# Linear attention, then SwiGLU: batch 0's values by plain loads with casts on chip, smaller first weight slices, and four tiny early reads

## The chip, the cores and the metric

The kernel runs on one core of a Trainium2 chip. Times are device microseconds of one execution of the whole program. A core has five engines with a queue of instructions each: TensorE (PE, with its weight loads shown apart as PEld), VectorE (DVE), ScalarE (ACT), GpSimd (POOL) and SyncE (SP). They run side by side and wait for one another by semaphores. Transfers are issued from the queues of SP, ACT and GpSimd and carried out by 16 DMA engines.

## What is computed

```python
# q, k, v: [8 batches, 8 heads, 576 tokens, 64], float32
q_s = softmax over the 64 of each row of q
k_s = softmax over the 576 tokens of k
kv = einsum('bhsd,bhse->bhde', k_s, v)
attn = einsum('bhsd,bhde->bhse', q_s, kv)
x = attn.transpose(0, 2, 1, 3).reshape(4608, 512)
g = x @ w_gate            # [512, 1536]
out = (g * sigmoid(g) * (x @ w_val)) @ w_out      # [1536, 512]
```

Only the exponentials are taken, without the maximum; the division by the row sum of q is done on q, the one by the column sum of k on the rows of kv.

## The kernel before

**Attention.** A batch is worked in two groups G of four heads. A tile of q, k or v of a group has 128 partitions: partition halves g = 0 and 1 hold head pairs, nine tokens of each head lie in one partition, and the two heads of a pair stand side by side, so a raw tile is 128 x 2 x 576. `load` (L72) brings one in as float32 on the SP queue. `exp_of` takes exponentials on ScalarE into bf16 (`eq`, `ek`); `norm_sum` and `norm_mul` make the normalised q (`qs`) on VectorE; `turn_pe` transposes `qs` on PE into PSUM (`tp`) and `turn_out` copies it out (`qt`). The nine token steps are cut in two pieces, `BANKS = ((0, 5), (5, 9))`, of 640 and 512 columns. `kv` is the sum over the nine steps of `ek` transposed times v; it is scaled into `kn`, and `x_mm` multiplies `kn` with `qt` into `xp`, which `x_out` copies into `xt`, the bf16 input of the feed-forward part, [128, 4, 4608].

**Feed-forward.** `m_unit` (L286) makes 128 of the 1536 hidden columns for one batch of tokens: matmuls of `wg` and of `wv` with `xt`, over four slices kk of the model dimension, then Silu on ScalarE (`sg`) and the product on VectorE (`hr`). For batch 0 the 576 tokens stand in two parts of 320 and 256. Slices kk = 0 and 1 of `xt` come from group 0, kk = 2 and 3 from group 1. `o_mm` multiplies `hr` with `wo` for 128 tokens, and the result is copied and stored.

**Order.** Inside `tc.manual_schedule()` (L353) the order of the code is the order of each engine's queue. The opening is written out by hand for batch 0 (L354 to L452):

- SP issues q and k of group 0, then q and k of group 1.
- GpSimd waits until k of group 0 has landed (the manual dependency of L359), then issues the loads of v, which cast float32 to bf16 on the way (`v16`; group 1 in two pieces of tokens). On the same queue follow the weight slices, casting too: columns 0 to 256, 256 to 640, 640 to 1024 and 1024 to 1536 of `wg` and `wv` in turn (L380), then four slices of `wo`.
- ScalarE takes the exponentials; VectorE the sums and the normalised q of group 0, then of group 1.
- PE first does matmuls on zeros (`spin`), which keep it busy, the sums of k over tokens (`key_sum`, whose reciprocal `kvr` VectorE takes), the transposes, `kv_first` (kv of batch 0, from `v16`), `x_mm`, and then the twelve `m_unit`s of batch 0 with PE work alone between them. In the first of these (`by_part`) all matmuls of the first 320 tokens stand ahead of those of the other 256.
- Batch 1's loads are released when the second slice of `wo` has landed (`w_dma[-3]`, L454), batch 2's as buffers come free.

After that the work goes in chunks of about 512 tokens, with the attention of a later batch placed between the `m_unit`s of an earlier one; there v is loaded as float32 on SP and cast on GpSimd (`cast_v`, L127). That part is the same in both kernels.

Of the kernel before, what the change touches and what calls it, by code (L numbers as in the profile page):

```python
# [15 lines left out]
def kernel(  # L16
# [10 lines left out]
    nc = tc.nc  # L27
# [26 lines left out]
    hr = const.tile([128, MT, RING], BF16, name="hr", tag="hr")  # L54
    ident = const.tile([128, 128], BF16, name="ident", tag="ident")
    sel = const.tile([128, 2], BF16, name="sel", tag="sel")
    zero = const.tile([128, 512], BF16, name="zero", tag="zero")
    vbs = [const.tile([128, T, 130], BF16, name=f"vb{i}", tag=f"vb{i}") for i in range(2)]
    v16 = [const.tile([128, 2, T * 64], BF16, name=f"v16_{i}", tag=f"v16_{i}") for i in range(2)]
# [2 lines left out]

    raw = {}

    def head_ap(src, b, G, t0=0, t1=T):
        return bass.AP(
            tensor=src.tensor,
            offset=src[b, 4 * G].offset + 64 * t0,
            ap=[[T * 64, 128], [2 * HSTR, 2], [1, (t1 - t0) * 64]],
        )  # L70

    def load(what, src, b, G, pieces=((0, T),), after=None):  # L72
        t_ = ld.tile([128, 2, T * 64], FP32, tag=what, name=what)
        raw[what, b, G] = t_
        last = None
        for t0, t1 in pieces:
            last = nc.sync.dma_start(out=t_[:, :, 64 * t0:64 * t1], in_=head_ap(src, b, G, t0, t1))
            if after is not None:
                tc.add_manual_dep(last.ins, after.ins.name, SYNC, reason="order of loads")
                after = None  # L80
        return last
# [61 lines left out]
        nc.vector.reciprocal(out=rr, in_=rs)  # L143
        return first

    def norm_mul(b, G, pieces=((0, T),), engs=None):
# [3 lines left out]
        for (t0, t1), eng in zip(pieces, engs or (nc.vector, nc.vector)):  # L150
            n = 2 * (t1 - t0)
            eng.tensor_mul(  # L152
                qs[:, t0:t1, :].rearrange("p t (h d) -> p (t h) d", d=64),
                eq2[:, 2 * t0:2 * t1, :],
                s["rr"][:, 2 * t0:2 * t1].to_broadcast([128, n, 64]),
            )
# [27 lines left out]
    def ek_of(b, G, g, t):  # L184
        return st[b, G]["ek"][64 * g:64 * g + 64, t, :, :].rearrange("p h d -> p (h d)")
# [49 lines left out]
    def x_one(b, G):  # L235
        for i in range(2):
            x_out(b, G, i, x_mm(b, G, i))
# [45 lines left out]

    def m_unit(c0, n, m, by_part=False):  # L286
        ms = slice(m * 128, (m + 1) * 128)
        parts = [(c0, n)] if n <= 512 else [(c0, 320), (c0 + 320, n - 320)]
        gu = []
        for nm in ("g_ps", "u_ps"):  # L290
            ps = [bank(nm) for _ in parts]
            gu.append(ps)
        steps = [(a, kk, i) for a in range(2) for kk in range(KT) for i in range(len(parts))]
        if by_part:
            steps.sort(key=lambda a: (a[2], a[0], a[1]))
        for a, kk, i in steps:
            c, w_ = parts[i]
            nc.tensor.matmul(  # L298
                out=gu[a][i][:, 0:w_], lhsT=(wg, wv)[a][:, kk, ms], rhs=xt[:, kk, c:c + w_],
                start=(kk == 0), stop=(kk == KT - 1),  # L300
            )
# [49 lines left out]

    make_identity(nc, ident)
    with tc.manual_schedule():  # L353
        kd = []  # L354
        for G in range(NG):
            load("q", q, 0, G)
            kd.append(load("k", k, 0, G))
        d = nc.gpsimd.dma_start(out=v16[0], in_=head_ap(v, 0, 0))  # L358
        tc.add_manual_dep(d.ins, kd[0].ins.name, SYNC, reason="order of loads")  # L359
        for t0, t1 in BANKS:  # L360
            nc.gpsimd.dma_start(out=v16[1][:, :, 64 * t0:64 * t1], in_=head_ap(v, 0, 1, t0, t1))  # L361

        warm = const.tile([128, 1], FP32, name="warm", tag="warm")
        nc.vector.memset(warm, 0.0)
# [11 lines left out]
        first = norm_sum(0, 0, BANKS)  # L376
        norm_mul(0, 0, BANKS)
        norm_sum(0, 1, BANKS)

        for c0, n in ((0, 256), (256, 384), (640, 384), (1024, 512)):  # L380
            w_slice(wg, moe_w_gate, c0, n)
            w_slice(wv, moe_w_val, c0, n)
        w_dma = [wo_slice(m0, 3) for m0 in (0, 3, 6, 9)]
# [17 lines left out]
            s["kvr"] = at.tile([128, 2], FP32, tag="kvr", name="kvr")  # L401
            nc.vector.reciprocal(out=s["kvr"], in_=ks[:, 0:2])

        def kv_first(G, t0=0, t1=T):
            s = st[0, G]
            if t0 == 0:
                s["kv"] = [bank("kv") for _ in range(2)]
            for t in range(t0, t1):
                for g in range(2):
                    r = slice(64 * g, 64 * g + 64)  # L410
                    nc.tensor.matmul(
                        out=s["kv"][g][:, 0:128].rearrange("p (h d) -> p h d", d=64),
                        lhsT=ek_of(0, G, g, t), rhs=v16[G][r, :, 64 * t:64 * t + 64],
                        start=(t == 0), stop=(t == T - 1),
                    )

        def scale_first(G, eng1):
            s = st[0, G]
            kn = s["kn"] = at.tile([128, 2, 128], BF16, tag="kn1", name="kn1")
            nc.scalar.mul(kn[:, 0, :], s["kv"][0][:, 0:128], s["kvr"][:, 0:1])  # L420
            if eng1 is nc.scalar:
                nc.scalar.mul(kn[:, 1, :], s["kv"][1][:, 0:128], s["kvr"][:, 1:2])
            else:
                nc.vector.tensor_scalar_mul(kn[:, 1, :], s["kv"][1][:, 0:128], s["kvr"][:, 1:2])

        spin(8)
        spin(6, first)
        key_sum(0)
        turn_pe(0, 0, 0)
        turn_pe(0, 0, 1)  # L430
        turn_out(0, 0, 0, nc.scalar)
        exp_of("k", 0, 1)
        turn_out(0, 0, 1, nc.scalar)
        norm_mul(0, 1, BANKS)
        spin(6)
        key_sum(1)
        kv_first(0)
        scale_first(0, nc.scalar)
        turn_pe(0, 1, 0)
        turn_pe(0, 1, 1)  # L440
        turn_out(0, 1, 0, nc.vector)
        turn_out(0, 1, 1, nc.vector)
        xp0 = x_mm(0, 0, 0), x_mm(0, 0, 1)
        kv_first(1, *BANKS[0])
        kv_first(1, *BANKS[1])
        x_out(0, 0, 0, xp0[0], (nc.scalar, nc.scalar))
        x_out(0, 0, 1, xp0[1], (nc.vector, None))
        scale_first(1, nc.vector)
        xp1 = x_mm(0, 1, 0), x_mm(0, 1, 1)
        x_out(0, 1, 0, xp1[0], (nc.scalar, nc.vector))  # L450
        x_out(0, 0, 1, xp0[1], (None, nc.vector))
        x_out(0, 1, 1, xp1[1], (nc.scalar, nc.vector))  # L452

        load_batch(1, w_dma[-3], by_group=True)  # L454
        load_batch(2)

        for m in range(MT):
            m_unit(0, S, m, by_part=(m == 0))

        exp_of("q", 1, 0)  # L460
        exp_of("k", 1, 0)
# [121 lines left out]
```

## Time and profile before

| | |
|---|---|
| time, median of 3 runs | 317.82 us (317.57 to 317.85) |
| the profiled execution | 317.75 us, span 316.0 us |
| PE busy | 304.7 us, 96% of the span |
| DVE, ACT, POOL busy | 52%, 47%, 9% |
| DMA moved | 45.75 MB, 145 GB/s on average |
| granted TensorE clock | 0.998 |

The span is the time from the first to the last instruction on the core, and somewhat shorter than the timed run. PE is busy in 96% of it, but matmuls are pipelined and their ends are modelled, so that "busy" is not "at its peak". In the page's 40 slices of 7.9 us PE is at 90% or more from the third slice to the last but one; the first two have 60 and 70%. What lies ahead of the third slice, the first 16 us, is the opening for batch 0 described above. DMA is busy at 70 to 90% of its share in the first seven slices, and clearly less later.

### The profile page before, as it was taken

Reading aid. Unit: us, or ns where it says so; the run is one execution under the profiler, and the core shown is the slowest. Engines: PE = TensorE matmul, PEld = TensorE weight load, DVE = VectorE, ACT = ScalarE, POOL = GpSimd, SP = SyncE. Lnnn points to the kernel's source line nnn. Section 1 sums busy time; section 2 is a strip of 40 time slices with the busy share of each in tenths; the row PEclk is TensorE's granted clock in tenths of the full one; section 3 lists DMA queues with packets and bytes.
Section 4 is the critical chain, followed back from the end, with each engine's and each line's share of the span. In section 5 each row is a group of like instructions: output and inputs, shape, how many; then the busy total and the mean of one; then the engine's idle time right before and its main releaser. Section 6 shows DMA issues by size and latency. Waiting matters only on the chain.

```text
span 316.0 us, 4856 instructions
## 1 busy us (share of the span) xinstructions
PE 304.7 (96%) x1865; PEld 152.0 (48%) x1894; DVE 163.2 (52%) x277; ACT 147.6 (47%) x218; POOL 28.0 (9%) x35
## 2 busy tenths in 40 slices
PE   6799999999999999999999999999999999999994
PEld 2477744554444444544454444544454444444443
DVE  3834476685754566455835492639354333423421
ACT  4743488634663465447354637355743113312300
POOL 2930021100200020002000200020000000000000
PEclk9999999999999999999999999999999999999999
DMA  7999999269246806490629253944310202020124
GB/s 269 183 204 207 296 393 391 68 160 364 50 91 179 338 17 128 112 394 11 141 68 352 97 110 66 322 162 103 66 41 0 65 3 66 0 68 3 31 68 102
DMA packets 39304, 45.75 MB, mean 145 GB/s; under 512 B 16368, under 2 KB 23024, under 8 KB 39280
## 3 DMA queue, kind: packets, MB, share of 16 engines
q1 hardware_dynamic: 32480, 39.99, 42.0%
q0 software_dynamic: 6640, 5.31, 10.9%
q8 instruction: 15, 0.25, 0.3%
q10 hardware_dynamic: 160, 0.13, 0.2%
q14 instruction: 9, 0.07, 0.1%
HBM read 37.75 MB, written 9.44 MB: 149 GB/s over the span
## 4 chain that ended last, share of the span: by engine, by line
PE 88%; DMA 4%; DVE 3%; ACT 2%; issue 1%; POOL 1%; SPq 0%; DVEq 0%
PE g_ps L298 29%; PE u_ps L298 29%; PE o_ps L322 25%; PE kv L191 3%; DMA wv<-in_moe_w_val_dram 2%; DMA k<-in_k_dram 2%; DVE rs L138 1%; PE xp L267 1%; DVE qs L152 1%; PE o_ps L342 1%; ACT L124 1%; ACT eq L124 1%; POOL v L361 0%; PE tp L166 0%; POOL v L358 0%
## 5 line engine op out<-in xcount | busy, mean ns | idle before, releaser
L305 ACT ACTIVATE sg<-g_ps 128x512 bf16<-128x512 f32 (+2 forms) x120 | 65.1, 554 | 139.1 <-PE g_ps L298 120.7
L306 DVE TENSOR_TENSOR hr<-sg,u_ps 128x512 bf16<-128x512 bf16 (+2 forms) x120 | 74.5, 630 | 87.8 <-PE u_ps L298 80.4
L298 PE MATMUL g_ps<-xt,wg 128*128 128x512 bf16 (+2 forms) x469 | 110.0, 358 | 1.0 <-ACT xt L111 0.2
L298 PE MATMUL u_ps<-xt,wv 128*128 128x512 bf16 (+2 forms) x468 | 109.8, 357 | 1.2 <-DMA wv<-in_moe_w_val_dram 0.5
L322 PE MATMUL o_ps<-wo,hr 128*128 128x512 bf16 x414 | 93.0, 379 | 0.4 <-issue 0.2
L298 PEld LDWEIGHTS <-wv 128*128 128x128 bf16 x480 | 46.9, 98 | 47.2 <-DMA wv<-in_moe_w_val_dram 0.9
L298 PEld LDWEIGHTS <-wg 128*128 128x128 bf16 x480 | 45.8, 98 | 45.3 <-issue 0.7
L322 PEld LDWEIGHTS <-hr 128*128 128x128 bf16 x420 | 40.9, 98 | 49.1
L113 DVE COPY o_sb<-o_ps 128x512 f32<-128x512 f32 x33 | 22.4, 680 | 39.2 <-PE o_ps L322 37.3
L127 POOL CAST vb<-v 128x1152 bf16<-128x1152 f32 x14 | 16.0, 1146 | 174.3 <-DMA v<-in_v_dram 111.8
L138 DVE TENSOR_REDUCE rs<-eq 128x18 f32<-128x1152 bf16 (+2 forms) x18 | 21.7, 1214 | 13.2 <-ACT eq L124 13.2
L152 DVE TENSOR_TENSOR qs<-eq,rr 128x1152 bf16<-128x1152 bf16 (+2 forms) x18 | 22.1, 1237 | 0.1
L124 ACT ACTIVATE eq<-q 128x1152 bf16<-128x1152 f32 (+2 forms) x18 | 18.1, 1050 | 4.5 <-DMA q<-in_q_dram 4.4
L124 ACT ACTIVATE ek<-k 128x1152 bf16<-128x1152 f32 x16 | 18.0, 1158 | 0.3 <-DMA k<-in_k_dram 0.2
L305 ACT ACT_TABLE_LOAD x12 | 15.4, 1283 | 0.2
L124 ACT ACT_TABLE_LOAD x11 | 14.1, 1283 | 0.2
L388 PE MATMUL idle<-zero 128*128 128x512 bf16 x20 | 6.1, 459 | 3.0 <-DVE rs L138 1.8
L191 PE MATMUL kv<-vb,ek 64*128 64x129 bf16 x252 | 8.7, 217 | 0.0
L191 PEld LDWEIGHTS <-ek 64*128 64x128 bf16 x252 | 7.3, 94 | 2.7 <-ACT sg L305 2.1
L275 ACT CAST xt<-xp 128x512 bf16<-128x512 f32 x12 | 6.4, 588 | 3.6 <-PE xp L267 3.6
L276 DVE CAST xt<-xp 128x512 bf16<-128x512 f32 x12 | 7.7, 683 | 0.0
L347 ACT COPY o_sb<-o_ps 128x128 f32<-128x128 f32 x2 | 0.5, 265 | 13.3 <-DVE o_sb L346 13.3
(46 smaller groups left out, 70.2 us busy)
## 6 DMA issues: line engine op xcount, KB each, us to landing
q<-in_q_dram SPq DMA_DIRECT2D x16, 576.0 KB, 5.6
k<-in_k_dram SPq DMA_DIRECT2D x16, 576.0 KB, 7.3
out_dram<-o_sb SPq DMA_DIRECT2D x70, 128.0 KB, 2.3
v<-in_v_dram SPq DMA_DIRECT2D x14, 576.0 KB, 9.0
wo<-in_moe_w_out_dram POOLq DMA_DIRECT2D x4, 384.0 KB, 16.3
wg<-in_moe_w_gate_dram POOLq DMA_DIRECT2D x2, 384.0 KB, 9.7
wv<-in_moe_w_val_dram POOLq DMA_DIRECT2D x2, 384.0 KB, 10.7
wg<-in_moe_w_gate_dram POOLq DMA_DIRECT2D x1, 512.0 KB, 13.7
```

The lines of the kernel that those rows point to most:

```text
L113: eng.tensor_copy(out=out, in_=in_)
L124: nc.scalar.activation(out=e[:, t0:t1], in_=src[:, t0:t1], func=AF.Exp)
L127: nc.gpsimd.tensor_copy(out=vbs[G][:, :, 0:128].rearrange("p t (h d) -> p t h d", d=64), in_=raw["v", b, G].rearrange("p h (t d) -> p t h ...
L138: i = nc.vector.reduce_sum(out=rs[:, 2 * t0:2 * t1], in_=eq2[:, 2 * t0:2 * t1, :], axis=mybir.AxisListType.X)
L152: eng.tensor_mul(qs[:, t0:t1, :].rearrange("p t (h d) -> p (t h) d", d=64), eq2[:, 2 * t0:2 * t1, :], s["rr"][:, 2 * t0:2 * t1].to_broadca ...
L191: nc.tensor.matmul(out=kv[g][:, c:c + 129], lhsT=ek_of(b, G, g, t), rhs=vbs[G][r, t, 0:129], start=(t == 0), stop=(t == T - 1),)
L275: nc.scalar.copy(out=xt[:, 2 * G, c0:c0 + 512], in_=main[G][0])
L276: nc.vector.tensor_copy(out=xt[:, 2 * G + 1, c0:c0 + 512], in_=main[G][1])
L298: nc.tensor.matmul(out=gu[a][i][:, 0:w_], lhsT=(wg, wv)[a][:, kk, ms], rhs=xt[:, kk, c:c + w_], start=(kk == 0), stop=(kk == KT - 1),)
L305: nc.scalar.activation(out=sg[:, 0:w_], in_=g_ps[:, 0:w_], func=AF.Silu)
L306: nc.vector.tensor_mul(hr[:, m, r:r + w_], sg[:, 0:w_], u_ps[:, 0:w_])
L322: nc.tensor.matmul(out=o_ps, lhsT=hr[:, m, r0:r0 + 128], rhs=wo[:, m, :], start=(m == 0), stop=(m == MT - 1),)
```

## The change

- **v of batch 0** is no longer cast by its DMA. Both groups come in as float32 on the SP queue, like q and k, in the order q0, k0, q1, v0, k1, v1; v1 comes head by head (`by_head`), in two transfers. Group 0 is cast by one copy on GpSimd, which stands ahead of the weight slices on that queue. Group 1 is cast by `cast_half`, one head at a time: 384 columns on VectorE and 192 on ScalarE.
- **Weight slices** of `wg` and `wv` are now columns 0 to 128, 128 to 256, 256 to 512, 512 to 1024 and 1024 to 1536: ten issues instead of eight.
- **Four tiny reads**, 16 rows of 16 numbers each of k, v, `w_gate` and `w_val`, are issued on the ScalarE queue ahead of everything else there. Their destination `touch` is read by nothing.
- **Order on the engines**: `key_sum` moves behind the first transposes (group 0) and behind those of group 1 (group 1); kv of group 1 is made head by head (`kv_first(1, 0, 1)` and `kv_first(1, 1, 2)`), each behind the cast of its half; `kn` of group 0 is scaled by ScalarE and VectorE, one half each, instead of by ScalarE alone; the copies of `xp` and `qt` stand in another order.
- **First `m_unit`**: the sort takes kk = 0 and 1 (both parts, `wg` and `wv`) ahead of kk = 2 and 3.

An argument of `norm_mul` that no call uses goes as well; that hunk is left out.

```diff
--- before
+++ after
@@ -54,6 +54,7 @@
     hr = const.tile([128, MT, RING], BF16, name="hr", tag="hr")
     ident = const.tile([128, 128], BF16, name="ident", tag="ident")
     sel = const.tile([128, 2], BF16, name="sel", tag="sel")
+    touch = const.tile([16, 4, 16], FP32, name="touch", tag="touch")
     zero = const.tile([128, 512], BF16, name="zero", tag="zero")
     vbs = [const.tile([128, T, 130], BF16, name=f"vb{i}", tag=f"vb{i}") for i in range(2)]
     v16 = [const.tile([128, 2, T * 64], BF16, name=f"v16_{i}", tag=f"v16_{i}") for i in range(2)]
@@ -62,19 +63,19 @@
 
     raw = {}
 
-    def head_ap(src, b, G, t0=0, t1=T):
+    def head_ap(src, b, G, h=(0, 2)):
         return bass.AP(
             tensor=src.tensor,
-            offset=src[b, 4 * G].offset + 64 * t0,
-            ap=[[T * 64, 128], [2 * HSTR, 2], [1, (t1 - t0) * 64]],
+            offset=src[b, 4 * G + 2 * h[0]].offset,
+            ap=[[T * 64, 128], [2 * HSTR, h[1] - h[0]], [1, T * 64]],
         )
 
-    def load(what, src, b, G, pieces=((0, T),), after=None):
+    def load(what, src, b, G, after=None, by_head=False):
         t_ = ld.tile([128, 2, T * 64], FP32, tag=what, name=what)
         raw[what, b, G] = t_
         last = None
-        for t0, t1 in pieces:
-            last = nc.sync.dma_start(out=t_[:, :, 64 * t0:64 * t1], in_=head_ap(src, b, G, t0, t1))
+        for h in ((0, 1), (1, 2)) if by_head else ((0, 2),):
+            last = nc.sync.dma_start(out=t_[:, h[0]:h[1], :], in_=head_ap(src, b, G, h))
             if after is not None:
                 tc.add_manual_dep(last.ins, after.ins.name, SYNC, reason="order of loads")
                 after = None
@@ -283,7 +284,7 @@
 
 
 
-    def m_unit(c0, n, m, by_part=False):
+    def m_unit(c0, n, m, first=False):
         ms = slice(m * 128, (m + 1) * 128)
         parts = [(c0, n)] if n <= 512 else [(c0, 320), (c0 + 320, n - 320)]
         gu = []
@@ -291,8 +292,8 @@
             ps = [bank(nm) for _ in parts]
             gu.append(ps)
         steps = [(a, kk, i) for a in range(2) for kk in range(KT) for i in range(len(parts))]
-        if by_part:
-            steps.sort(key=lambda a: (a[2], a[0], a[1]))
+        if first:
+            steps.sort(key=lambda a: (a[1] // 2, a[2], a[0], a[1]))
         for a, kk, i in steps:
             c, w_ = parts[i]
             nc.tensor.matmul(
@@ -351,14 +352,18 @@
 
     make_identity(nc, ident)
     with tc.manual_schedule():
-        kd = []
-        for G in range(NG):
-            load("q", q, 0, G)
-            kd.append(load("k", k, 0, G))
-        d = nc.gpsimd.dma_start(out=v16[0], in_=head_ap(v, 0, 0))
-        tc.add_manual_dep(d.ins, kd[0].ins.name, SYNC, reason="order of loads")
-        for t0, t1 in BANKS:
-            nc.gpsimd.dma_start(out=v16[1][:, :, 64 * t0:64 * t1], in_=head_ap(v, 0, 1, t0, t1))
+        load("q", q, 0, 0)
+        load("k", k, 0, 0)
+        load("q", q, 0, 1)
+        load("v", v, 0, 0)
+        load("k", k, 0, 1)
+        load("v", v, 0, 1, by_head=True)
+        for i, src in enumerate((k, v, moe_w_gate, moe_w_val)):
+            row = src.shape[-1] if len(src.shape) == 2 else 8 * T * 64
+            nc.scalar.dma_start(
+                out=touch[:, i, :],
+                in_=bass.AP(tensor=src.tensor, offset=src[(0,) * len(src.shape)].offset, ap=[[row, 16], [1, 16]]),
+            )
 
         warm = const.tile([128, 1], FP32, name="warm", tag="warm")
         nc.vector.memset(warm, 0.0)
@@ -376,8 +381,9 @@
         first = norm_sum(0, 0, BANKS)
         norm_mul(0, 0, BANKS)
         norm_sum(0, 1, BANKS)
-
-        for c0, n in ((0, 256), (256, 384), (640, 384), (1024, 512)):
+        nc.gpsimd.tensor_copy(out=v16[0], in_=raw["v", 0, 0])
+
+        for c0, n in ((0, 128), (128, 128), (256, 256), (512, 512), (1024, 512)):
             w_slice(wg, moe_w_gate, c0, n)
             w_slice(wv, moe_w_val, c0, n)
         w_dma = [wo_slice(m0, 3) for m0 in (0, 3, 6, 9)]
@@ -401,61 +407,62 @@
             s["kvr"] = at.tile([128, 2], FP32, tag="kvr", name="kvr")
             nc.vector.reciprocal(out=s["kvr"], in_=ks[:, 0:2])
 
-        def kv_first(G, t0=0, t1=T):
+        def kv_first(G, h0=0, h1=2):
             s = st[0, G]
-            if t0 == 0:
+            if h0 == 0:
                 s["kv"] = [bank("kv") for _ in range(2)]
-            for t in range(t0, t1):
+            for t in range(T):
                 for g in range(2):
                     r = slice(64 * g, 64 * g + 64)
                     nc.tensor.matmul(
-                        out=s["kv"][g][:, 0:128].rearrange("p (h d) -> p h d", d=64),
-                        lhsT=ek_of(0, G, g, t), rhs=v16[G][r, :, 64 * t:64 * t + 64],
+                        out=s["kv"][g][:, 64 * h0:64 * h1].rearrange("p (h d) -> p h d", d=64),
+                        lhsT=ek_of(0, G, g, t), rhs=v16[G][r, h0:h1, 64 * t:64 * t + 64],
                         start=(t == 0), stop=(t == T - 1),
                     )
 
-        def scale_first(G, eng1):
+        def cast_half(h):
+            n = 64 * 6
+            nc.vector.tensor_copy(out=v16[1][:, h, 0:n], in_=raw["v", 0, 1][:, h, 0:n])
+            nc.scalar.copy(out=v16[1][:, h, n:], in_=raw["v", 0, 1][:, h, n:])
+
+        def scale_first(G):
             s = st[0, G]
             kn = s["kn"] = at.tile([128, 2, 128], BF16, tag="kn1", name="kn1")
             nc.scalar.mul(kn[:, 0, :], s["kv"][0][:, 0:128], s["kvr"][:, 0:1])
-            if eng1 is nc.scalar:
-                nc.scalar.mul(kn[:, 1, :], s["kv"][1][:, 0:128], s["kvr"][:, 1:2])
-            else:
-                nc.vector.tensor_scalar_mul(kn[:, 1, :], s["kv"][1][:, 0:128], s["kvr"][:, 1:2])
+            nc.vector.tensor_scalar_mul(kn[:, 1, :], s["kv"][1][:, 0:128], s["kvr"][:, 1:2])
 
         spin(8)
         spin(6, first)
+        turn_pe(0, 0, 0)
         key_sum(0)
-        turn_pe(0, 0, 0)
         turn_pe(0, 0, 1)
         turn_out(0, 0, 0, nc.scalar)
+        turn_out(0, 0, 1, nc.scalar)
         exp_of("k", 0, 1)
-        turn_out(0, 0, 1, nc.scalar)
         norm_mul(0, 1, BANKS)
         spin(6)
-        key_sum(1)
         kv_first(0)
-        scale_first(0, nc.scalar)
         turn_pe(0, 1, 0)
+        scale_first(0)
         turn_pe(0, 1, 1)
         turn_out(0, 1, 0, nc.vector)
+        key_sum(1)
+        cast_half(0)
+        xp0 = x_mm(0, 0, 0), x_mm(0, 0, 1)
         turn_out(0, 1, 1, nc.vector)
-        xp0 = x_mm(0, 0, 0), x_mm(0, 0, 1)
-        kv_first(1, *BANKS[0])
-        kv_first(1, *BANKS[1])
-        x_out(0, 0, 0, xp0[0], (nc.scalar, nc.scalar))
-        x_out(0, 0, 1, xp0[1], (nc.vector, None))
-        scale_first(1, nc.vector)
-        xp1 = x_mm(0, 1, 0), x_mm(0, 1, 1)
-        x_out(0, 1, 0, xp1[0], (nc.scalar, nc.vector))
-        x_out(0, 0, 1, xp0[1], (None, nc.vector))
-        x_out(0, 1, 1, xp1[1], (nc.scalar, nc.vector))
+        kv_first(1, 0, 1)
+        x_out(0, 0, 0, xp0[0])
+        cast_half(1)
+        kv_first(1, 1, 2)
+        scale_first(1)
+        x_out(0, 0, 1, xp0[1])
+        x_one(0, 1)
 
         load_batch(1, w_dma[-3], by_group=True)
         load_batch(2)
 
         for m in range(MT):
-            m_unit(0, S, m, by_part=(m == 0))
+            m_unit(0, S, m, first=(m == 0))
 
         exp_of("q", 1, 0)
         exp_of("k", 1, 0)
```

More of the change, by code (lines that the diff above doesn't have):

```diff
@@ L144, in norm_sum, with norm_mul @@
         return first
-    def norm_mul(b, G, pieces=((0, T),), engs=None):
+    def norm_mul(b, G, pieces=((0, T),)):
         s = st[b, G]
@@ L149, in norm_mul @@
         qs = s["qs"] = at.tile([128, T, 128], BF16, tag="qs", name="qs")
-        for (t0, t1), eng in zip(pieces, engs or (nc.vector, nc.vector)):
+        for t0, t1 in pieces:
             n = 2 * (t1 - t0)
-            eng.tensor_mul(
+            nc.vector.tensor_mul(
                 qs[:, t0:t1, :].rearrange("p t (h d) -> p (t h) d", d=64),
```

## Prediction

> **What bounds the kernel now.** I read the chain of work that ended last first. On the page PE has 88% of it and DMA 4%: nearly the whole span is matmul after matmul, and an edit of the opening can only shift the moment from which that stream runs without gaps. So I asked for the same chain in order of time (start, us, what), over the first 20 us:
>
> ```profile
> 1.27 4.79 DMA k<-in_k_dram
> 6.05 0.30 issue
> 6.36 0.86 POOL v L358
> 7.21 1.43 POOL v L361 x2
> 8.64 0.74 POOL wg L99
> 9.38 6.77 DMA wv<-in_moe_w_val_dram
> 16.15 0.05 issue
> 16.20 0.72 PE u_ps L298 x4
> ```
>
> The first matmuls with wv wait for their weights. GpSimd holds its queue until k of group 0 has landed (6.06), issues three loads of v and then wg and wv, and wv lands at 16.15. After that PE is never idle: the timeline puts the first matmul of unit m=1 at 17.63, and from there each m takes 2 x 0.98 us. **17.63 is the number to compare with.**
>
> Second, the timelines by engine, to see how far behind that DMA the attention of batch 0 is (start, us, engine, line, op, tile, shapes, count, idle before):
>
> ```profile
> 8.94 1.41 DVE L138 TENSOR_REDUCE rs<-eq 128x10 f32<-128x640 bf16 x2 [0.38 <-ACT eq L124]
> 10.38 0.27 DVE L143 RECIPROCAL rr<-rs 128x18 f32<-128x18 f32 x1
> 10.57 0.11 DVE L402 RECIPROCAL kvr<-ks 128x2 f32<-128x2 f32 x1
> 10.69 1.43 DVE L152 TENSOR_TENSOR qs<-eq,rr 128x640 bf16<-128x640 bf16 x2
> 12.03 0.16 DVE L402 RECIPROCAL kvr<-ks 128x2 f32<-128x2 f32 x1
> ...
> 14.38 0.45 PE L220 MATMUL xp<-qt,kn 64*64 64x320 bf16 x8 [0.44 <-DVE kn L424]
> 14.87 0.79 PE L298 MATMUL g_ps<-xt,wg 128*128 128x320 bf16 x4
> 16.20 0.72 PE L298 MATMUL u_ps<-xt,wv 128*128 128x320 bf16 x4 [0.54 <-DMA wv<-in_moe_w_val_dram]
> ```
>
> VectorE works without a gap from 8.94 to 12.12; the last attention matmuls end at 14.83. Hence without any wait for weights the 16 matmuls of m=0 (1.96 us) would bring m=1 to 16.85. That is the most the weights can give, 0.8 us, and only if attention ends no later than now.
>
> Third, the times from issue to landing of the first loads: 3.9, 4.8, 6.4 and 7.3 us for q and k of groups 0 and 1, that is 4.6, 6.1, 8.2 and 9.6 on the clock. In batch 1, with only plain loads behind one another, they land 1.4 to 1.6 us apart. Last, the windows: DMA moves 350 to 410 GB/s while plain loads run, and 119 to 190 from 10 to 14 us, where casting loads of v and the first weights run; their bytes are counted after the cast, so 205 in the steady stretch is 410 of fp32. The queue is full from 2 us on.
>
> [...] L152 with 1152 columns takes 1.34 to 1.36 us, but 1.76 where the cast of L127 runs beside it (47.27, cast at 46.67). [...] the trace has weight packets of 512 B and up only (about 190 GB/s at 512 B, 207 at 1 KB).
>
> **The change part by part.** Clock of the before span, 316.0 us.
>
> *Loads.* The three casting v loads leave GpSimd (0.86+1.43 us of issue, and the wait for k). SP now issues q0, k0, q1, v0, k1, and v1 in two halves. The listing of instructions shows waits for reused semaphores: k1 for the first tiny read, the first half of v1 for q0 (4.6), the other half for a tiny read. They queue only k1 and v1 on SP, whose data come after 9 us anyway: nothing. From 4.63 in steps of 1.48: k0 6.1, q1 7.6 (was 8.2), v0 9.1, **k1 10.55 (was 9.6)**, v1 11.3 and 12.0.
>
> *Tiny reads.* Four issues on ScalarE ahead of its table load. Nearest row: a DMA issue on ACT, 0.50 to 0.56 us. 0.73+4x0.53+1.28+0.20 = 4.3, before q0 lands (4.63): nothing on the path; at 0.6 each or less still nothing. What they may save is not to be seen in the trace; [...] of which I take 0.
>
> *GpSimd.* The cast of v0 (1.15, row L127) runs 9.15 to 10.3, and the ten weight issues (0.78 each) queue behind it: wg starts at 10.3 instead of 8.63. The first v packets came 1.8 us after their issue, so weights flow from 12.1, about when SP's loads end. The first four slices are now 128 columns, 256-B packets. Packets of 512, 768 and 1024 B took 42, 59 and 76 ns per engine, a line through which gives 26 ns (estimate), or 0.83 us a slice, against 42 ns and 1.36 us if a small packet costs as much as a 512-B one. With 0.83 and 0.5 us of landing: wg and wv for m=0 at 13.4 and 14.3, m=1 at 15.9, the 256-column slices at 18.6, the next at 23.7. PE needs them at 15.9, 17.9, 20.8 and 24.7 (below). **The wait for wv is gone**, and the second wo slice, which releases batch 1's loads, lands at 32.6 instead of 33.2; PE waits for those loads nowhere now (ScalarE does at 43.6, for 1.1 us), so nothing more for it.
>
> *VectorE's order.* This becomes the path. The row sum of q1 follows qs of group 0, which ends at 8.56: start 8.60 (was 8.94). The four steps above take their 3.18: 11.78. Then kn of group 0, 0.35 (row L424): 12.15; first half of qt, 0.49: 12.6. The reciprocal of the key sum waits for exp of k1 (10.58 + 1.16 = 11.74), four transposes and the nine sums of PE (12.5): 12.75. Cast of half of v1, 384 columns: no row. Lower end 0.35 [...], upper end 0.57 (fp32 320 columns in 0.49, 1.14 ns for each more); I take 0.45: 13.2. Second half of qt 0.41, xt 0.49, second cast 0.45: 14.55, less 0.2 for overlapping neighbours (two copies of 0.49 and 0.42 show as 0.82): **14.35**. ScalarE's shares of the casts (192 columns, 0.3 from row L124's slope) are done by 13.8.
>
> *PE.* kv of the second half waits for that cast: 18 matmuls, 0.65: 15.0. kn and its semaphore, as now, 0.44: 15.44; eight xp matmuls 0.45: **15.9 (was 14.83)**. The sixteen of m=0, now sorted so that group 0's half goes first, hide the copies of xt (done by 16.7): 1.96 after a 0.04 handover, m=1 at 17.9.
>
> *Sum.* 17.9 - 17.63 = +0.25 us. The M phase, the exps after it and all else follow PE one for one. Span 316.25; the profiled run was 317.75 and the median 317.82, so the forecast is **318.1 us**: the attention chain takes back what the weights gave. Within 0.2% (0.64 us) counts as no change, about what a measurement of this kernel can tell.
>
> **Rivals.**
> A. *VectorE takes longer* (slower). [...] the qs product of group 1 blocked by GpSimd's cast if v0 lands after 9.3 (+0.4, the 1.76 above), k1 landing late by the lag that q1 shows now (8.2 against 7.6): together +0.8, 318.8. For it: no slack on VectorE from 8.6 to 14.3. It decides once the second cast ends after 14.75. Against: three things have to come together.
> B. *Small weight packets* (slower). At 1.36 us a slice the first four take 2.1 us more: the third slice of wv lands at 25.8, PE wants it at 24.7, and batch 1's loads come 1.5 us later, costing some 0.4 there: 319.5. It decides where a slice takes over 1.1 us. [...] against: the line through three packet sizes.
> C. *Attention keeps its pace* (faster). If VectorE and PE overlap more tightly, so that xp ends at 15.0 as now, m=1 starts at 17.0: 317.1. For it: q1 half a microsecond earlier, a v1 that lands at 12.0 instead of 13.5. Against: the durations of VectorE's own rows sum past it.
> D. *The tiny reads don't do what they say* or hold up q0 in the queue: +0.5 us, 318.4.
>
> **How the numbers follow.** Forecast 0.55, A 0.18, B 0.08, C 0.14, D 0.05. Faster by over 0.2%: 0.12 of C. Slower: 0.15 of A, 0.08 of B, 0.05 of the forecast and 0.02 of D, 0.30. Within: 0.58. Range 317.0 to 319.2: the forecast, A with its spread, D and most of C; B and the edge of C are left out.
>
> **What would show it.** Right: no PE wait for wv before u_ps; xp of group 1 ending near 15.9, with kv waiting for VectorE's cast; m=1 at 17.9; q1 near 7.6 and k1 near 10.6. Wrong: xp ending before 15.2 (C), any wait for wg or wv in m=0 to m=5 (B), the second cast ending after 14.75 (A), q0 landing after 4.8 (D). A gain of over 0.6 us would make the account of VectorE's queue wrong.

## The result, and the profile after

The changed kernel takes 320.55 us, the median of four executions (320.13 to 321.11), against 317.75 us (317.57 to 317.85, now with a fourth execution) for the kernel before. The ratio is 1.009, with an interval of 1.0071 to 1.0109: **slower by 2.8 us**, above the range of the forecast. The profiled execution took 320.13 us with a span of 318.3 us (before: 317.75 and 316.0). It lost 2.4 us, of which 2.3 lie inside the span.

Where are they? In the timeline of TensorE the first down-projection matmul (o_ps) of chunk 0 starts at 41.33 us, before at 39.19: +2.1. The first gate matmuls of chunk 1 are at 55.63 against 53.39: +2.2, and the distance stays near that to the end. So nearly all of it arises before 41 us, in the opening and in the M phase of chunk 0 (its twelve `m_unit`s). Landings in us, with what the prediction said:

| | before | predicted | after |
|---|---|---|---|
| q0 / q1 | 4.6 / 8.2 | 4.63 / 7.6 | 4.5 / 8.4 |
| v0 / k1 | 11.0 / 9.6 | 9.1 / 10.55 | 9.9 / 11.4 |
| first weight issue (GpSimd) | 8.63 | 10.3 | 11.06 |
| wg and wv for m=0 | 14.8, 16.2 | 13.4, 14.3 | 14.4, 16.0 |
| wg and wv for m=1 | with m=0 | 15.9 (both) | 16.7, 18.3 |
| wv for m=4 (column 512 on) | 20.4 | 23.7 | 26.6 |
| wv up to column 1024 | 24.3 | 23.7 | 26.6 |
| second wo slice, then batch 1's loads | 33.2 | 32.6 | 36.0 |

The row for m=4 shows what the cut points do. Before, column 512 came with the slice of columns 256 to 640; now it comes with 512 to 1024 and waits for the last byte of that larger slice.

The chain of work that ended last, for the changed kernel, in order of time (start, us, what):

```profile
2.28 7.64 DMA v<-in_v_dram
...
9.97 1.14 POOL v L384
11.12 0.84 POOL wg L100
...
19.29 16.69 DMA wo<-in_moe_w_out_dram
...
37.50 8.36 DMA q<-in_q_dram
...
45.88 1.17 ACT eq L125
```

Read it backwards: ScalarE's exp of q of batch 1 waits for its load until 45.86, which is 37.50 + 8.36 (before: 43.6). That load was held until the second slice of wo had landed at 35.98 (19.29 + 16.69). The slice stood in GpSimd's queue behind all of wg and wv, these behind the cast of v0 (L384), and the cast waited for v0 until 9.92 (2.28 + 7.64). In the chain before, the wait was for k0, at 6.06, and three issues stood between it and wg.

The chain names one road only. The windows of the changed kernel show two more (columns: stretch, its length, busy us and instruction count of PE, PEld, DVE, ACT and POOL, then granted TensorE clock, DMA share, GB/s):

```profile
11.00:12.00 1.00, 0.97 (x22) 0.74 (x22) 1.00 (x2) 0.55 (x1) 1.00 (x3) 1.00 0.36 131
12.00:13.00 1.00, 0.85 (x22) 0.66 (x20) 1.00 (x3) 1.00 (x3) 1.00 (x2) 1.00 0.25 25
13.00:14.00 1.00, 0.75 (x29) 0.54 (x27) 0.97 (x5) 0.75 (x3) 1.00 (x2) 1.00 1.36 128
14.00:15.00 1.00, 0.45 (x26) 0.32 (x18) 0.61 (x2) 0.03 (x1) 1.00 (x3) 1.00 1.55 146
15.00:16.00 1.00, 0.56 (x16) 0.23 (x10) 0.73 (x3) 0.71 (x3) 1.00 (x2) 1.00 1.66 159
16.00:17.00 1.00, 1.00 (x5) 0.55 (x6) 0.78 (x2) 0.98 (x3) 1.00 (x2) 0.51 1.23 132
17.00:18.00 1.00, 1.00 (x6) 0.66 (x5) 0.00 (x0) 0.92 (x1) 1.00 (x3) 0.50 1.14 116
...
19.00:20.00 1.00, 1.00 (x9) 0.73 (x7) 0.56 (x2) 0.38 (x1) 1.00 (x2) 0.79 1.39 166
```

The kernel before, in some of the same stretches:

```profile
12.00:13.00 1.00, 1.00 (x21) 0.75 (x17) 0.66 (x4) 0.62 (x2) 1.00 (x2) 1.00 1.16 119
...
14.00:15.00 1.00, 0.58 (x9) 0.27 (x10) 0.55 (x2) 0.57 (x2) 0.59 (x1) 1.00 1.43 193
15.00:16.00 1.00, 0.66 (x4) 0.20 (x2) 0.94 (x3) 0.98 (x3) 0.74 (x1) 1.00 1.36 198
```

The last column: SP's plain loads are over within 11 to 12 us, and from 12 to 13 DMA moves 25 GB/s, nearly nothing (before: 119), although all 4.72 MB of GpSimd's queue 0, the weights, are still to come (3 x 512 x 1536 numbers at 2 bytes, so bytes are counted after the cast; their first issue was at 11.06); then the weights come at 116 to 166 GB/s until 20 us (before: 183 to 218). The third figure from the right: from 16.0 to 19.4 us TensorE is granted **half its clock** (0.50). Its page has the dip in one digit, which the page before has not:

```profile
PEclk9979999999999999999999999999999999999998
```

TensorE's timeline in the changed kernel shows what the half clock hits (start, us, engine, line, operation, tile, shapes, count, idle before):

```profile
14.67 0.44 PE L417 MATMUL kv<-v,ek 64*128 64x64 bf16 x18 [0.55 <-DVE v L425]
15.54 0.45 PE L221 MATMUL xp<-qt,kn 64*64 64x320 bf16 x8 [0.44 <-ACT kn L431]
15.93 0.67 PE L299 MATMUL g_ps<-xt,wg 128*128 128x320 bf16 x2
...
19.57 1.14 PE L299 MATMUL g_ps<-xt,wg 128*128 128x320 bf16 x8
```

Attention ends at 15.99 and m=0 follows without a gap, but its sixteen matmuls take from 15.93 to 19.57, 3.6 us, and m=1 starts 1.9 us after the 17.63 of before. None of them waits for wv, and the prediction's first sign of being right ("no PE wait for wv before u_ps") is there. A sign of its rival B is there too: m=4's matmuls with wv start at 26.62, 0.2 us late, for the slice that landed at 26.6. VectorE's timeline in the changed kernel:

```profile
9.21 1.41 DVE L139 TENSOR_REDUCE rs<-eq 128x10 f32<-128x640 bf16 x2 [0.71 <-ACT eq L125]
...
13.18 0.45 DVE L425 CAST v<-v 128x384 bf16<-128x384 f32 x1
...
14.27 0.34 DVE L425 CAST v<-v 128x384 bf16<-128x384 f32 x1
15.16 0.35 DVE L432 TENSOR_SCALAR kn<-kv,kvr 128x128 bf16<-128x128 f32 x1 [0.55 <-PE kv L417]
```

It works through the queue that the prediction listed. It starts late, at 9.21 (predicted 8.60), since ScalarE's exp of q1 waits for its load, and the second cast ends at 14.61 (14.27 + 0.34).

So three delays of almost the same size lie side by side. Half clock gives m=1 at 19.57. Late weights: at full clock PE would have wanted the wv of m=4 near 24.7, and it landed at 26.6. Late loads of batch 1: they are released 2.7 us later. In this one trace TensorE itself loses 1.94 us up to m=1, 0.2 at the wv of m=4 and 0.1 between the first o_ps and chunk 1. But what a delay would cost without the others one trace cannot tell, since each hides the others; the experiments had to take them away one by one and together.

### The profile page after: what moved, and what is told of

It reads as the page before. It is cut to its first block, busy times and chain, and to the rows that moved or that the text cites. A ratio compares the mean times of both kernels' runs of the same rounds, so it can differ in the third digit from the quotient of the medians.

```text
span 318.3 us, 4936 instructions
## 1 busy us (share of the span) xinstructions
PE 309.6 (97%) x1912; PEld 153.3 (48%) x1912; DVE 164.2 (52%) x280; ACT 147.9 (46%) x219; POOL 28.4 (9%) x35
## 3 DMA queue, kind: packets, MB, share of 16 engines
q0 software_dynamic: 6880, 4.72, 10.2%
## 4 chain that ended last, share of the span: by engine, by line
PE 82%; DMA 10%; POOL 3%; DVE 1%; SPq 1%; ACT 1%; issue 0%
PE o_ps L323 26%; PE g_ps L299 26%; PE u_ps L299 26%; DMA wo<-in_moe_w_out_dram 5%; DMA q<-in_q_dram 3%; DMA v<-in_v_dram 2%; PE kv L192 2%; POOL wg L100 1%; POOL wv L100 1%; PE xp L268 1%; SPq L78 1%; PE o_ps L343 1%; DVE qs L153 1%; DVE rs L139 0%; ACT eq L125 0%; POOL v L384 0%
## 5 line engine op out<-in xcount | busy, mean ns | idle before, releaser
L306 ACT ACTIVATE sg<-g_ps 128x512 bf16<-128x512 f32 (+2 forms) x120 | 65.2, 554 | 140.0 <-PE g_ps L299 132.9
L299 PE MATMUL g_ps<-xt,wg 128*128 128x512 bf16 (+2 forms) x480 | 112.8, 360 | 0.2 <-ACT xt L112 0.2
L299 PE MATMUL u_ps<-xt,wv 128*128 128x512 bf16 (+2 forms) x480 | 112.4, 360 | 0.0
L299 PEld LDWEIGHTS <-wg 128*128 128x128 bf16 x480 | 46.1, 98 | 45.5 <-issue 0.9
L128 POOL CAST vb<-v 128x1152 bf16<-128x1152 f32 x14 | 16.1, 1148 | 175.5 <-DMA v<-in_v_dram 136.6
L139 DVE TENSOR_REDUCE rs<-eq 128x18 f32<-128x1152 bf16 (+2 forms) x18 | 21.7, 1215 | 13.5 <-ACT eq L125 13.5
L394 PE MATMUL idle<-zero 128*128 128x512 bf16 x20 | 7.8, 554 | 2.6 <-DVE rs L139 1.4
```

The lines of the kernel that those rows point to most:

```text
L128: nc.gpsimd.tensor_copy(out=vbs[G][:, :, 0:128].rearrange("p t (h d) -> p t h d", d=64), in_=raw["v", b, G].rearrange("p h (t d) -> p t h ...
L139: i = nc.vector.reduce_sum(out=rs[:, 2 * t0:2 * t1], in_=eq2[:, 2 * t0:2 * t1, :], axis=mybir.AxisListType.X)
L299: nc.tensor.matmul(out=gu[a][i][:, 0:w_], lhsT=(wg, wv)[a][:, kk, ms], rhs=xt[:, kk, c:c + w_], start=(kk == 0), stop=(kk == KT - 1),)
L394: i = nc.tensor.matmul(out=idle, lhsT=zero[:, 0:128], rhs=zero, start=True, stop=True)
```

## The experiments

Each is compared with the kernel before, timed anew in the same session (317.43, 317.46 and 317.56 us). "Loss" is against that.

**First group: the changed kernel with one suspect removed.** *Run 1* keeps TensorE busy in its gaps with idle matmuls on zeros, in bank columns that are unused or written anew afterwards: two and four ahead of the halves of kv of group 1, three ahead of its xp.

```diff
+    def fill(out, n):
+        for _ in range(n):
+            nc.tensor.matmul(
+                out=out, lhsT=zero[:, 0:128], rhs=zero[:, 0:out.shape[-1]], start=True, stop=True
+            )
...
-        kv_first(1, 0, 1)
+        kv_first(1, 0, 1, 2)
...
-        kv_first(1, 1, 2)
+        kv_first(1, 1, 2, 4)
...
-        x_one(0, 1)
+        for i in range(2):
+            x_out(0, 1, i, x_mm(0, 1, i, 3 if i == 0 else 0))
```

> The changed kernel, with nine idle matmuls on zeros more in PE's gaps between 13.4 and 15.5 us (two and four ahead of the two kv halves of group 1, three ahead of the xp matmuls of group 1). Theory: two delays of nearly the same size lie side by side at the attention of batch 1, the half TensorE clock in m=0 and the loads of batch 1 that are released 2.7 us later. Then the granted clock stays 1.0 at 16 to 19.5 us, m=1 starts near 17.9 instead of 19.57, but q of group 1 of batch 1 still lands near 45.9, and the time stays at 320.2 to 320.6. Rival, the clock alone makes the loss: 318.6 to 319.0. If the clock stays at half although PE is busy, the gaps aren't its cause.

Measured: 320.28 us (319.69 to 320.41), ratio 1.0084 (1.0071 to 1.0097), loss 2.85. The clock stays full (0.997 to 1.0 in the five executions) and m=1 starts at 18.26 instead of 19.57. Yet nothing is gained, and its TensorE timeline says why (the matmuls of m_unit are on L306 in this kernel):

```profile
24.41 1.14 PE L306 MATMUL g_ps<-xt,wg 128*128 128x320 bf16 x8
26.50 1.15 PE L306 MATMUL u_ps<-xt,wv 128*128 128x320 bf16 x8 [0.95 <-DMA wv<-in_moe_w_val_dram]
```

TensorE arrives early and waits 0.95 us for wv, which lands at 26.5 as before the edit. The half clock had been hiding a wait for weights.

*Run 2* undoes only the slicing of wg and wv.

```diff
-        for c0, n in ((0, 128), (128, 128), (256, 256), (512, 512), (1024, 512)):
+        for c0, n in ((0, 256), (256, 384), (640, 384), (1024, 512)):
```

> The changed kernel with the weight slices of before (columns 0-256, 256-640, 640-1024, 1024-1536). Theory (two delays side by side): the second wo slice lands 1.5 to 2.5 us earlier, at 33.5 to 34.5 instead of 36.0, the half clock in m=0 stays, and the time falls by only 0.2 to 0.5, to 320.1 to 320.4. Rival, the small packets and the late release make the whole loss: 318.0 to 318.6. If weights flow no faster than now while GpSimd issues, packet size is not what slows them.

Measured: 320.74 us (318.93 to 323.04), ratio 1.0113 (1.0077 to 1.0148), loss 3.3. The first wv slice, now 256 columns, lands at 18.2, and its TensorE timeline has the wait that the small slices were free of:

```profile
18.23 0.71 PE L299 MATMUL u_ps<-xt,wv 128*128 128x320 bf16 x2 [1.75 <-DMA wv<-in_moe_w_val_dram]
```

In that idle time the clock fell to half (0.50), from 16.9 to 23.7 us. The one execution with a mean granted clock of 1.0 took 318.93, the two with 0.988 and 0.989 took 322.82 and 323.04. The second wo slice landed at 35.5, not at the expected 33.5 to 34.5: the slices alone don't bring the weights back.

*Run 3* is runs 1 and 2 together.

> Both edits together: idle matmuls in PE's gaps, and the weight slices of before. Theory (two delays side by side): now the loss goes, 318.2 to 318.9. Rivals: if the clock alone counts, the same as with the idle matmuls alone; if the release alone counts, the same as with the slices alone.

Measured: 319.54 us (319.12 to 319.73), ratio 1.0062 (1.005 to 1.0074), loss 2.1, with full clock (1.0) in every execution. The expectation was missed: wv of m=0 still came at 17.0 (a wait of 0.61 us) and the second wo slice at 34.9. Something other than clock and slices holds the weights; the next suspect is their late start.

*Run 4* removes the four tiny reads from the changed kernel.

```diff
-        for i, src in enumerate((k, v, moe_w_gate, moe_w_val)):
...
-            nc.scalar.dma_start(
...
```

> The changed kernel without the four tiny reads. Theory: they lie on no path, 320.3 to 320.9, as the changed kernel (320.55). Rival, [...] k and v land up to 0.5 us later and the time rises to 321 or more. Rival, their semaphores hold up k and v of group 1: faster by 0.3 or more.

Measured: 319.53 us (319.45 to 320.19), ratio 1.0069 (1.0057 to 1.0081), loss 2.1, where the changed kernel had 2.8 in another session. v0 landed at 9.6; but in other executions with the tiny reads it came between 9.0 and 10.0, so that landing proves nothing of them. The wait for wv at 26.4 is there, and the half clock too (15.8 to 19.2).

**Second group: start and release.** *Run 5* is run 3 with the first slices of wg and wv issued as soon as q1 has landed, ahead of the cast of v0:

```diff
-        nc.gpsimd.tensor_copy(out=v16[0], in_=raw["v", 0, 0])
...
+            d = w_slice(wg, moe_w_gate, c0, n)
             w_slice(wv, moe_w_val, c0, n)
+            if c0 == 0:
+                tc.add_manual_dep(d.ins, q1.ins.name, SYNC, reason="order of loads")
+                nc.gpsimd.tensor_copy(out=v16[0], in_=raw["v", 0, 0])
```

> The changed kernel with idle matmuls in PE's gaps and the weight slices of before, and in addition the first slice of wg and of wv issued on GpSimd as soon as q of group 1 has landed (about 8.2 us), ahead of the cast of v of group 0 instead of behind it. Theory: the rest of the loss is that DMA stands nearly still from 11.2 to 12.8 us, because the weights queue behind that cast. Then DMA stays busy, the second wo slice lands near 33.3 instead of 34.9, m=1 starts near 18.0, and the time is 317.6 to 318.4 (319.54 without this edit). Rival, the weights that flow earlier hold back k and v of group 1, and xp ends later by as much: 319 or more.

Measured: 318.60 us (318.26 to 318.98), ratio 1.0033 (1.002 to 1.0045), loss 1.1. The windows of this kernel, columns as above:

```profile
12.00:13.00 1.00, 0.85 (x21) 0.66 (x22) 0.97 (x3) 0.58 (x3) 1.00 (x2) 1.00 1.44 191
13.00:14.00 1.00, 1.00 (x28) 0.46 (x26) 1.00 (x4) 0.68 (x2) 1.00 (x3) 1.00 1.44 196
...
15.00:16.00 1.00, 1.00 (x29) 0.51 (x21) 0.67 (x2) 0.63 (x2) 1.00 (x2) 1.00 1.25 191
16.00:17.00 1.00, 1.00 (x16) 0.72 (x9) 0.83 (x3) 0.89 (x3) 0.95 (x2) 1.00 1.33 205
```

and two of run 3:

```profile
15.00:16.00 1.00, 1.00 (x22) 0.41 (x13) 0.69 (x3) 0.68 (x3) 1.00 (x2) 1.00 1.39 131
16.00:17.00 1.00, 0.41 (x6) 0.07 (x2) 0.81 (x2) 0.98 (x3) 1.00 (x3) 1.00 0.97 137
```

The hole of 12 to 13 us (25 GB/s in the changed kernel, 53 in run 3) is filled with 191, and the 512-B packets go on at 196. A second dip is gone as well: run 3 has 131 and 137 from 15 to 17 us, this run 191 and 205. Together the two explain why the second wo slice lands 2.4 us earlier although the first weight bytes move only 1.1 us earlier (11.2 instead of 12.3); what makes the second dip is not shown. wv up to column 1024 lands at 23.2, the second wo slice at 32.5, TensorE waits for no weights, and the M phase ends at 39.63 against 39.19 before. Idle matmuls, the slices of before and the early start together take away most of the loss.

*Run 6* asks whether the late loads of batch 1 cost by themselves: run 1 with them released by the first wo slice instead of the second.

```diff
-        load_batch(1, w_dma[-3], by_group=True)
+        load_batch(1, w_dma[-4], by_group=True)
```

> The changed kernel with idle matmuls in PE's gaps, and the loads of batch 1 released by the first slice of wo instead of the second. Theory (with the clock at full rate, the late release is what is left): q and v of group 1 of batch 1 land 1.5 to 2 us earlier and the time falls from 320.28 to 318.6 to 319.1. Rival, the loads then only share the queue with the rest of wo and land no earlier: 320.0 to 320.5.

Measured: 320.24 us (319.99 to 321.24), ratio 1.0089 (1.0075 to 1.0102), loss 2.8: nothing gained, the rival held. The loads were released at 33.8 instead of 36.2, but q of group 1 still landed at 45.8 (46.1) and v at 49.8 (49.7). Its chain:

```profile
16.22 10.38 DMA wv<-in_moe_w_val_dram
...
36.29 13.54 DMA v<-in_v_dram
```

The earlier release makes the transfers of group 1 longer (from issue to landing q takes 10.5 us and v 13.5, in run 1 8.2 and 10.7); the rest of wo is still being moved then, as the rival had it: DMA moves 214, 303 and 340 GB/s in the three steps of 1.5 us from 36 to 40.5 us, and 393 only behind them (208, 271 and, from 39 us on, 403 in the changed kernel). The road through wv is in the same chain.

The traces price the late loads in another way: by TensorE's time from the first o_ps of chunk 0 to the first gate matmul of chunk 1, where it needs batch 1. It is 14.20 us before, 14.30 in the changed kernel, 14.58 in run 1, 14.43 in run 3, 14.21 in this run, and 14.04 in run 5. So, as far as single traces tell, the late loads cost 0.1 us in the changed kernel and some 0.4 in run 1. In its trace this run saves those 0.4, but its wv came as late as before (26.6), and the median shows no gain.

*Run 7* does the opposite in the kernel before: release by the third wo slice.

```diff
-        load_batch(1, w_dma[-3], by_group=True)
+        load_batch(1, w_dma[-2], by_group=True)
```

> The kernel before, with the loads of batch 1 released by the third slice of wo instead of the second: about 2 us later, nothing else. It measures the price of a late release by itself. Theory: 319.0 to 319.5 (317.43 without). Rival, there is slack at batch 1: under 318.

Measured: 318.35 us (317.9 to 319.34), ratio 1.0021 (1.0009 to 1.0034), loss 0.9. Release 1.6 us later, q of group 1 at 44.0 instead of 43.6: nearly half of the delay is slack. By the measure of run 6 TensorE takes 14.74 us to chunk 1 instead of 14.20. The price was over-estimated, but the loads do sit at the edge.

*Run 8* adds only the tiny reads to the kernel before.

> The kernel before, with the four tiny reads on the ScalarE queue and nothing else. Without them the changed kernel was faster by about 0.7 us of its loss. If they cost by themselves (loads of q and k held up on the DMA queues): 317.8 to 318.4. [...] If they do nothing: 317.3 to 317.6.

Measured: 317.68 us (317.13 to 318.46), ratio 1.0005 (0.9995 to 1.0015): no difference that can be told. In its trace q0 landed at 4.9 and k of group 1 at 10.3 (4.6 and 9.6 without), so a small hold-up of the loads is not ruled out by this one execution; in the time it doesn't show.

**Third group: each delay with the other removed.** *Run 9* is run 5 without the idle matmuls.

> The changed kernel with the weight slices of before and their first pair issued ahead of the cast of v, but without the idle matmuls. It measures the half clock by itself once no weight is late. Theory (late weights are the cause, and the half clock is hidden behind them in the changed kernel): where the clock halves in m=0 the time is 319.5 to 320.3, against 318.6 with the idle matmuls; where the gaps fall so that it doesn't, about 318.4. Rival, the clock costs nothing anywhere: 318.3 to 318.8 in every run.

Measured: 319.69 us (318.2 to 320.15), ratio 1.0052 (1.0031 to 1.0073), loss 2.1. Its windows in the profiled execution:

```profile
13.00:14.00 1.00, 0.44 (x18) 0.32 (x18) 1.00 (x4) 0.57 (x2) 1.00 (x2) 1.00 1.45 198
14.00:15.00 1.00, 0.46 (x21) 0.34 (x21) 0.45 (x3) 0.44 (x2) 1.00 (x2) 1.00 1.28 196
...
16.00:17.00 1.00, 1.00 (x7) 0.65 (x5) 0.21 (x1) 0.98 (x2) 0.57 (x1) 0.50 1.34 215
```

Busy for 0.44 and 0.46 of two microseconds, then half clock, with attention ending at 15.43 and m=1 only at 18.88. The executions of this kernel split by their mean granted clock: 0.991 to 0.993 took 319.49, 319.89, 320.04 and 320.15 us; 0.997 and 1.0 took 318.20 and 318.55. The mean doesn't say where in an execution the clock was low, but in the profiled one (0.993) it was m=0. With the weights on time the half clock costs about 1.5 us, where in the changed kernel the times don't follow the clock (0.992 took 320.13, 0.998 took 321.11, 1.0 took 320.25).

*Run 10* is run 5 with the slices of the change (128, 128, 256, 512, 512).

> The changed kernel with idle matmuls and with its own slices (columns 0-128, 128-256, 256-512, ...), the first pair issued ahead of the cast of v. Against 318.6 with the old slices in the same place it measures the packets of 256 and 512 B by themselves. Theory: the four small slices take about 1.3 us each instead of 0.65, the third slice of wv lands near 25.5 and PE waits for it; 319.2 to 320. Rival, an early start is all that counts: 318.2 to 318.8.

Measured: 318.88 us (318.24 to 320.03), ratio 1.0039 (1.0025 to 1.0052), loss 1.3. With runs 1, 3 and 5 it makes a square, all four with the idle matmuls; in each field the landing of wv up to column 1024, of the second wo slice, and the loss:

| | slices of the change | slices of before |
|---|---|---|
| weights behind the cast | run 1: 26.5, 36.1, 2.85 | run 3: 25.2, 34.9, 2.1 |
| first pair ahead of the cast | run 10: 25.7, 34.6, 1.3 | run 5: 23.2, 32.5, 1.1 |

The early start takes off 1.0 to 1.5 us, the slices of before 0.2 to 0.75; the 0.2 (run 10 against run 5) lies within the noise. "Slices" are packet size and cut points at once: with those of before, m=4's wv comes with columns 256 to 640, at 21.2 in run 3 and 19.5 in run 5, so that TensorE does not wait there. The square can't part the two. The expected 319.2 to 320 was missed: the wv of m=4 lands at 25.7, near the expected 25.5, but PE waits only 0.18 us for it.

A part of each time lies outside the trace. Time minus span is 1.7 to 2.0 us in every execution of the kernel before, of the changed kernel and of runs 1, 4, 6 and 10, but 2.1 to 2.2 in every one of runs 2, 3, 5, 9 and 11, the changed kernel with the slices of before. So these slices cost about 0.35 us outside the span; why is open (run 12, the kernel before with one issue less, has 2.0 to 2.2 as well). Inside it the four fields lose, by their median spans, 2.9 (run 1), 1.8 (run 3), 1.3 (run 10) and 0.8 (run 5).

*Run 11* is run 5 without the tiny reads.

> The kernel of the early weights and idle matmuls (318.6) without the four tiny reads. If the reads cost by themselves as they seemed to in the changed kernel: 317.9 to 318.2. If they lie on no path: 318.4 to 318.8.

Measured: 318.35 us (317.97 to 318.69), ratio 1.0022 (1.0014 to 1.003), 0.25 less than run 5, which lies within the noise, and between the two expectations.

*Run 12* looks for a version that beats the kernel before: there, v of group 1 as one casting load instead of two, so that the weights start one issue earlier.

```diff
-        for t0, t1 in BANKS:
-            nc.gpsimd.dma_start(out=v16[1][:, :, 64 * t0:64 * t1], in_=head_ap(v, 0, 1, t0, t1))
+        nc.gpsimd.dma_start(out=v16[1], in_=head_ap(v, 0, 1))
```

> The kernel before, with v of group 1 loaded by one casting transfer (packets of 1152 B) instead of two (640 and 512 B). Theory: [...] the weights then land 0.5 to 0.7 us earlier, m=1 starts by as much earlier, and the time is 316.8 to 317.2, faster than both kernels. Rival, v of group 1 lands later and holds back kv: 317.5 or more.

Measured: 317.91 us (317.42 to 318.86), ratio 1.0009 (1.0 to 1.0018): not faster. The weights are issued from 7.9 but land at 14.7 and 16.1 as before. v's packets are of 1152 B here, so packets of 640 and 512 B are not shown to hold the weights back in the kernel before. That the same bytes of v stand ahead of them is the likely reason; it was not tested. No run beat the kernel before.

## Why the prediction was wrong, step by step

**Loads.** Within the spread of executions. v0 came at 9.9 against 9.1, k1 at 11.4 against 10.55; run 9, with the same loads, had q1 at 7.6, v0 at 9.0 and k1 at 10.5. This is not where it failed: in run 1 the cast started at 9.38 and the weight issues at 10.46, close to the predicted 9.15 and 10.3, and the loss was the same.

**Tiny reads.** On ScalarE they are hidden (issued from 0.74 to 2.64 us), and q0 was not held up in the changed kernel (4.5): rival D falls as it was put. Added to the kernel before they cost nothing measurable in time (run 8); taken out of run 5 they give 0.25 us, within the noise. The difference of 0.7 between run 4 and the changed kernel is across sessions. Between 0 and 0.7 stays open, and no run shows a mechanism.

**GpSimd: the first step that failed.** The start was right where v0 came as predicted: in run 1 the first weight packet moves at 12.06 (12.1), following its issue by 1.6 us and not by 1.8. What failed is the time of the first six weight slices, "0.83 us a slice" for the small ones. From the landing of the first to that of wv up to column 512 the prediction has 5.2 us (13.4 to 18.6). It took 7.1 us in the changed kernel (14.4 to 21.5), 7.6 in run 1 (13.8 to 21.4) and 7.2 in run 10 (13.4 to 20.6). A small slice took 1.3, 1.6 and 0.9 us in them. From there to wv up to column 1024 it took the predicted 5.1 us in all three. So the wv of m=4, predicted for 23.7 and wanted at 24.7, came at 26.6, and the second wo slice at 36.0 instead of 32.6. With its margin of 1.0 us used up, the later start that the prediction took for free has a price too: starting the first pair ahead of the cast is worth 1.0 to 1.5 us (the square). Rival B named the place, the sign and the size of that delay (2.1 us more, third wv at 25.8; 319.5 us for the whole) and was given 0.08.

Its reason, the small packets, is shown in part only. From 14 to 16 us, where the changed kernel moves nothing but 256-B packets, it has 146 and 159 GB/s, not far from the 158 that 0.83 us for a slice of 128 KB means; the shortfall comes from 16 to 19 us (116 to 135), where the 256-column slices begin, and run 3, whose weights have no packet under 512 B, dips there as well. In that stretch every trace has one transfer of 16 KB on another queue (queue 8, "instruction", from 16.1 us in the changed kernel, 0.9 us long, 2.0 in run 1); whether it holds up a slice was not tested. Outside these dips the rates rise with packet size: 146 and 159 GB/s at 256 B, 191 and 196 at 512 B (run 5, 12 to 14 us), 206 at 1 KB (the changed kernel, 25 to 35 us); the price in time, together with that of the cut points, is 0.2 to 0.75 us (the square).

**VectorE and attention.** Right at its end, in part by luck. The path began 0.6 us late (row sum of q1 at 9.21, predicted 8.60), because q1 landed at 8.4 instead of 7.6, and then took 5.4 us to the end of the second cast instead of 5.75. That cast ended at 14.61 (14.35), the casts took 0.45 and 0.34 us (0.45 taken; the lower end, 0.35, was the author's estimate, and a line through bf16 copies of 640 and 512 columns in the kernel before, 0.492 and 0.415 us, gives 0.34 for 384), kv started at 14.67, attention ended at 15.99 (15.9). In run 9, where q1 came at 7.6, attention ended at 15.43. Rivals A (second cast after 14.75) and C (xp before 15.2) fall. Of A's parts, the qs product of group 1 lay beside the cast of v0 for 0.16 us (10.95 to 11.11) and took 1.44 us, where group 0's took 1.43 with no cast beside it; a later one of 1152 columns with 0.54 us of a cast beside it (49.52) took 1.75.

**PE: the second step that failed.** "1.96 after a 0.04 handover" for m=0 took the full clock for granted; it was 3.6 us at half clock. The prediction did not consider the clock at all. At full clock the figure is right: 1.97 us in run 1 (16.29 to 18.26). Runs 1 and 9 show that the thin stretch ahead of m=0 is the cause: from 13 to 16 us TensorE is busy for 0.75, 0.45 and 0.56 of each microsecond in the changed kernel, and for 1.00 of each in run 1; the traces with its gaps filled keep 1.0. The size is 1.5 us in run 9, and nothing in the changed kernel, where late weights lie behind it.

**Why the sum is 2.8 and not more.** The two failed steps lie side by side. Clock alone cured: 2.85 (run 1). Weights alone cured: 2.1 (run 9). Both: 1.1 (run 5), and 0.8 without the tiny reads (run 11). Of the 1.1 that remain in run 5, about 0.35 lie outside the span and go with its slices. Inside, its m=1 is at 18.07 against 17.63, +0.44. Most of this is the idle matmuls' own: VectorE waits 0.90 us for kv ahead of kn, 0.55 in the changed kernel. The rest is open. The late loads of batch 1 cost by themselves 0.9 us in run 7 and, by the traces, 0.1 in the changed kernel.

## What to carry to other kernels

When work is moved onto an engine that also issues DMAs, ask what stands behind it in that queue, down to the last transfer: a later start, or slower first transfers, are carried to the end of the stream, even where the first transfers come in time (here wg for m=0 at 14.4 instead of 14.8, the second wo slice at 36.0 instead of 33.2). Where two delays lie side by side, removing either alone shows little or nothing, and only removing both shows what each is worth (here losses of 2.85 and 2.1 with one removed, 1.1 with both). Before costing matmuls at their usual duration, look how full TensorE is in the microseconds ahead of them, and with what (here 0.63 of 3.4 us, with narrow matmuls, and then 3.6 us for what takes 1.97 at full clock).

## What was not expected of the hardware

The granted clock fell to half for 3.4 us (16.0 to 19.4) in the changed kernel, after a stretch of the same length in which TensorE was busy for 2.17 us, or 0.63. It was not idle: its longest gap there was 0.55 us. These are windows cut on the 3.4-us steps of each trace's clock record: first that of the changed kernel, then one each of run 10 and of the kernel before, where the clock stayed at 1.0 afterwards:

```profile
12.60:16.02 3.42, 2.17 (x66) 1.49 (x65) 2.73 (x10) 1.92 (x8) 3.42 (x6) 1.00 1.41 132
8.40:11.82 3.42, 2.14 (x30) 1.23 (x29) 2.71 (x6) 2.75 (x5) 3.16 (x4) 1.00 1.11 373
3.92:7.33 3.41, 1.58 (x8) 0.51 (x6) 1.88 (x4) 2.42 (x3) 0.97 (x2) 1.00 1.04 380
```

So the busy share alone doesn't decide: 0.63 and even 0.46 kept the clock there. What differs is the kind of work, 66 mostly narrow matmuls (2 to 320 columns) against 30 and 8, among them those on zeros of 512 columns; no run separates it from other reasons. The half clock lasts 3.4 us here and in runs 4 (15.8 to 19.2) and 9 (15.7 to 19.1), and twice that in run 2 (16.9 to 23.7). Executions of one kernel fall to both sides (run 9: a mean clock of 0.991 to 0.993 in four, 0.997 and 1.0 in two); why is not shown. Nine idle matmuls, 1.9 us of work in gaps, kept the clock at 1.0 in all five executions of run 3. Of the 39 executions with them (runs 1, 3, 5, 6, 10 and 11) 38 have a mean clock of 0.997 or more; one of run 6, for which there is no trace, has 0.994.
